# Where the V tiles live, when V and the expert weights load, and one score unit per slot: a fused attention and mixture-of-experts kernel

## The chip, the cores and the metric

The kernel runs on one core of a Trainium2 chip. The metric is device time in microseconds (us) of one execution. The core has TensorE (matmuls; PE, with PEld for its weight loads), VectorE (DVE), ScalarE (ACT), GpSimd (POOL) and SyncE (SP). Each works through its own instructions in order, and they wait for each other and for DMAs on semaphores. A DMA that GpSimd, ScalarE or SyncE issues is carried out by 16 DMA engines that all share.

## The reference

Block-causal attention for 8 batches of 8 heads, 576 positions and 64 dimensions (blocks of 64), whose output (4608 tokens of 512) goes through a mixture of 8 experts, of which each token takes two, by noisy logits:

```python
scores = scale * np.matmul(q, k.transpose(0, 1, 3, 2))
mask = block_i >= block_j
scores = np.where(mask, scores, -1000000000.0)
attn = np.exp(scores - np.max(scores, axis=-1, keepdims=True))
attn = attn / (np.sum(attn, axis=-1, keepdims=True) + 1e-09)
x = np.matmul(attn, v)          # then heads side by side, (4608, 512)
...
noisy_logits = x @ w_gate + np.log1p(np.exp(x @ w_noise)) * noise
top2 = np.argpartition(-noisy_logits, 2, axis=1)[:, :2]
top2_w = softmax of the two logits
...
for e in range(E):
    for k in range(2):
        mask = top2[:, k] == e
        h = np.maximum(x[mask] @ w1[e], 0.0)
        out[mask] += top2_w[mask, k, None] * (h @ w2[e])
```

w1 is 8 x 512 x 1024 and w2 is 8 x 1024 x 512; inputs and output are float32, the kernel's matmuls bfloat16.

## The kernel before

**Attention in groups and slots.** The 8 batches are taken two at a time, in 4 groups (g = 0 to 3), both batches of a group in the two halves of the partitions. A group is cut into UG = 26 slots: 13 score units for heads 0 to 3 (set 0) and 13 for heads 4 to 7 (set 1). A score unit (`score_unit`, L285) is a few matmuls of keys with queries into one of two PSUM buffers, and one exp by ScalarE (L302, or L313 for the last unit of a set) that empties it. Beside the score units, each slot has a list of other work, written down by hand: `at(slot, fn, ...)` puts a function into a slot, and `run(slot)` emits what stands there. The order of the program is the order on each engine. In a slot can stand the transposes of q and k of this group or the next (`transpose_qk`, copied out by VectorE or ScalarE), the products of exps and V (`av_tile`, L324, copied out by VectorE), the transposes of the finished rows (`x_transpose`), a router step (`router_step`), a load, or a scatter. In the loop of L794 the even slots emit two score units and then their own work, the odd slots only their work.

**V.** `load_v` (L210) loads V of a group into one of two tiles, `vt[g % 2]`, ten loads for a group, issued by GpSimd in slots 9 to 18 of the group before. The tiles have a column of ones (L722) that yields the sum of the exps. `xrs[g]` (L328), the finished rows of a group, comes from `xr_pool`, which has three buffers.

**Router and scatter.** For each group the router finds the two experts and a slot number for each token. `scatter` (L496) then writes the rows to a table in DRAM ordered by expert, xd[half], 18 indirect DMAs for a group, all issued by GpSimd; groups 0 and 1 make half 0, groups 2 and 3 half 1. The scatters of groups 0 to 3 stand in slots 52 to 63, 78 to 95, 101 to 114 and 118 to 135. Each is tied to a recent instruction (`pace[-1]`), so that they don't come too early.

**Experts.** From slot 104 on 16 blocks follow: one block is one half and one expert (`SEQ`, L627), 640 rows. Its rows come by a transposing DMA that SyncE issues (`load_x`, L515), which waits for all 36 scatters of that half. `layer1(b, fb)` (L567) is 8 steps of 8 matmuls and a relu by ScalarE; `layer2(b, c)` (L581) is 5 tiles of 8 matmuls. What a half's earlier experts contributed is stored to DRAM (yd, by a DMA that ScalarE issues) and gathered again later (`gather`, L609, GpSimd), added, and scattered to the output (L598). Layer 1, step 0, of block b + 1 stands before layer 2 of block b. With E1 = 4 the order is half 0 with experts 0 to 3, half 1 with experts 0 to 3, and then by turns, half 0 and half 1, with expert 4, 5, 6, 7. `XL` (L847) says in which step the rows of a later block are loaded, `WL` (L823) in which step a piece of an expert's weights; each step is followed by one `run(slot)` (slots 111 on).

**Weights.** An expert's weights are four DMAs of 512 KB (`load_w`, L220, k = 0 to 3), issued by GpSimd. Experts 0 and 1 go to the two buffers of `wE`, expert 2 to `wM`, expert 3 to `wL`. Expert 0 stands in slots 53 to 59, expert 1 in slots 80 to 92, expert 2 in slots 112 to 120, expert 3 in slots 124 to 133 (L811); experts 4 to 7 follow in the blocks. So on GpSimd's queue, from slot 52 on, all scatters, eight V loads and two half ones, and the weights of experts 0 to 3 stand one behind another.

Of the kernel before, what the change touches and what calls it, by code (L numbers as in the profile page):

```python
# [19 lines left out]
def kernel(  # L20
# [12 lines left out]
    nc = tc.nc  # L33
# [149 lines left out]
    kv = k.rearrange("b h s d -> (b h s d)").rearrange("(t p c) -> p t c", p=P, c=512)  # L183
    raws = {}
    vt = [v_pool.tile([P, TG, H, D + 1], BF16, name=f"vt{i}") for i in range(2)]
    hq = hq_pool.tile([P, 2 * FB * CAP], BF16)
    qT = hq[:, 0:73 * 64]
    kT = hq[:, 73 * 64:2 * 73 * 64]
# [20 lines left out]

    def load_v(g, idx, p0, n, tok):  # L210
        b, s0 = divmod(tok, S)
        nc.gpsimd.dma_start(out=vt[g % 2][p0:p0 + n, idx, :, 0:D],  # L212
                            in_=v[b, :, s0:s0 + n, :].rearrange("h s d -> s h d"))

    def v_loads(g):
# [107 lines left out]

    def av_tile(g, st, idx, part=None):  # L324
        esc, esc4 = escs[(g, st)]
        vb = vt[g % 2]
        if g not in xrs:
            xrs[g] = xr_pool.tile([P, TG, DR], BF16, tag="xr", name="xr")  # L328
            nc.gpsimd.memset(xrs[g][:, :, Dm + 2 * NREC:DR], 0.0)
            nc.gpsimd.tensor_copy(xrs[g][:, :, Dm + 4:Dm + 6].bitcast(I32)[:, :, 0], tokm[:, g, :])  # L330
        xr = xrs[g]
        if part != 1:
            avs_open[idx] = av_ps.tile([P, SET, D + 1], F32, tag="av", name="av")
        av = avs_open[idx]
        heads = range(SET) if part is None else range(2 * part, 2 * part + 2)
        if idx < 8:
            hf, ib = divmod(idx, 4)
            for hh in heads:
                for jt in range(ib + 1):
                    c = EO[jt] + (ib - jt) * P  # L340
                    nc.tensor.matmul(out=av[:, hh, :], lhsT=esc[:, hh, hf, c:c + P],  # L341
                                     rhs=vb[:, 4 * hf + jt, st * SET + hh, :], start=(jt == 0), stop=(jt == ib))
# [280 lines left out]
    GS = (2, 3, 5, 6)  # L623


    E1 = 4
    SEQ = [(h, e) for h in range(NH) for e in range(E1)]  # L627
    for e in range(E1, E):
        SEQ += [(0, e), (1, e)]
# [71 lines left out]
    def read_flags():  # L701
        rs["over"] = nc.values_load(flag_i[0:1, 0:1], min_val=0, max_val=1)

    pools = {}

    def load_later(e, k):
        load_w(pools["wL"], e, k)

    fl = keep.tile([P, 4, E], F32)
    flm = keep.tile([P, 1], F32)  # L710
    flag_i = keep.tile([P, 1], I32)
# [6 lines left out]
    nc.vector.tensor_copy(ident, ident_f)  # L718
    load_qk(0, (1,))
    load_nz()  # L720
    for i in range(2):
        nc.vector.memset(vt[i][:, :, :, D:D + 1], 1.0)  # L722
    load_qk(0, (2, 3))
    setup_pool()
# [9 lines left out]
    for g in range(NG):  # L734
# [6 lines left out]
        if not last:  # L741
            for nm, ch, i in (("q", 0, 14 if g else 19), ("k", 0, 17 if g else 22), ("q", "4B", 22), ("k", "4B", 21)):
                at(s0 + i, transpose_qk, g + 1, nm, ch)
            for i, (fn, *a) in enumerate(v_loads(g + 1)):
                at(s0 + 9 + i, fn, *a)
        if g == 0:
            at(s0 + 13, load_qk, 1, (2,))
            at(s0 + 16, load_qk, 1, (3,))
# [40 lines left out]
    at(UG + 4, clear_x, 0, UG + 3)  # L789
    at(2 * UG + 4, clear_x, 1, 2 * UG + 3)  # L790
    for k in range(4):
        at(2 * UG + 1 + 2 * k, load_w, wE, 0, k)
        at(3 * UG + 2 + 4 * k, load_w, wE, 1, k)
    for u in range(NG * UG):  # L794
        if u % 2 == 0:
            score_unit(*divmod(u, UG))
            score_unit(*divmod(u + 1, UG))
        run(u)
        if u == 3 * UG + 13:
            raws_up.close()  # L800
            ffn["x"] = raws_up.enter_context(tc.tile_pool(name="xgp", bufs=3, side="right", reuse_waits="tile"))
            ffn["rec"] = raws_up.enter_context(tc.tile_pool(name="recp", bufs=1, side="right", reuse_waits="tile"))
            wM = raws_up.enter_context(tc.tile_pool(name="wM", bufs=1, side="right", reuse_waits="tile"))
            at(3 * UG + 18, load_x, 0)
            at(3 * UG + 19, load_x, 1)
            at(3 * UG + 20, load_rec, 0)
            at(3 * UG + 21, load_x, 2)
            at(3 * UG + 22, load_x, 3)
            for k in range(4):
                at(4 * UG + (8, 10, 13, 16)[k], load_w, wM, 2, k)  # L810
                at(4 * UG + (20, 23, 26, 29)[k], load_later, 3, k)  # L811

    WL = {}

    def open_top(slot):
        if slot == NG * UG + 6:
            top.close()
            wL = pools["wL"] = top.enter_context(tc.tile_pool(name="wL", bufs=2, reuse_waits="tile"))
            ffn["y"] = top.enter_context(tc.tile_pool(name="yp", bufs=4, reuse_waits="tile"))
            ffn["yg"] = [ffn["y"].tile([P, Dm], BF16, name=f"yg{i}", bufs=1) for i in range(GB)]  # L820
            for i, pool in enumerate((wL, wE, wE, wM)):
                for k in range(4):
                    WL[4 + 2 * i + k // 2, (2, 6)[k % 2]] = (pool, 4 + i, k)  # L823

    slot = NG * UG
    at(slot + 14, read_rec, 0)
# [16 lines left out]
    for i in range(7):  # L843
        run(slot)
        slot += 1
        open_top(slot)
    XL = {(b, 1): b + 2 for b in range(2, NB - 2)}  # L847
    for fn, b, j in steps:
        fn(b, j)
        if fn is layer1:  # L850
            if (b, j) in XL:
                load_x(XL[b, j])
            if (b, j) == (3, 1):
                load_rec(1)
            if (b, j) == (4, 3):
                read_rec(1)
            if (b, j) in WL:
                load_w(*WL[b, j])
            if b in (1, E1 + 1) and j == 1:
                gather(b, 0)  # L860
            elif b < 2 * E1 and j in GJ and GJ.index(j) < LT[SEQ[b][1]]:
                gather(b, GJ.index(j))
            if 2 * E1 <= b + 1 < NB and j in GS and GS.index(j) < LT[SEQ[b + 1][1]]:
                gather(b + 1, GS.index(j))
        if fn is layer2 and 2 * E1 <= b + 1 < NB and j == order(b)[0] and LT[SEQ[b + 1][1]] > 4:
            gather(b + 1, 4)
            if b + 1 == NB - 1:
                nc.gpsimd.drain()  # L868
# [93 lines left out]
```

## Time and profile before

| | us |
|---|---|
| median of 14 runs | 457.01 |
| lowest and highest of them | 444.27, 475.29 |
| the profiled execution | 445.26 |
| its span, first to last instruction | 443.5 |
| mean granted TensorE clock in it | 0.96 |

The page tells of one execution: how long each engine was busy, in which stretches, and what it waited for. A line of the timeline has the start, the length, the engine, the line of the kernel, the operation, the tiles it writes and reads, how many were merged, and in brackets the idle time of the engine before it and what ended it. A group of instructions is written like this (busy time and mean ns of one, then idle time before it and its releaser):

```profile
L577 ACT ACTIVATE hq<-hp 128x640 bf16<-128x640 f32 x128 | 89.9, 703 | 64.5 <-PE hp L574 59.0
L302 ACT ACTIVATE esc<-sc 128x1024 bf16<-128x1024 f32 x96 | 92.5, 1023 | 11.0 <-PE sc L299 10.6
L499 POOL DMA_INDIRECT xd<-xr,slots x72 | 71.6, 994 | 31.6 <-issue 13.9
L212 POOL DMA_DIRECT2D vt<-in_v_dram x40 | 34.0, 874 | 9.6 <-PE av L355 5.1
```

The attention fills the span up to about 152 us, the 16 blocks of the experts the rest.

### The profile page before, as it was taken

What the parts mean: (1) busy time and instruction counts of PE and PEld (TensorE: products, weight loads), DVE (VectorE), ACT (ScalarE), POOL (GpSimd) and SP (SyncE); (2) the same over time, 40 slices, a digit from 0 to 9 for tenths busy, and PEclk for the clock granted to TensorE, in tenths of its full rate; (3) what the DMA queues carried; (4) which work ended last, traced back from release to release, by engine and by line L of the source; (5) the groups of instructions that cost most, each with busy time, mean ns of one, the idle gap of its engine ahead of it and who ended that gap; (6) DMA issues with size and microseconds to landing.
All of it is one profiled execution on the core that took longest, in us unless ns stands there. A gap on an engine that the chain in (4) does not pass through costs nothing. (4 is left out here: it accounts for less than half of the span.)

```text
span 443.5 us, 9826 instructions
## 1 busy us (share of the span) xinstructions
PE 402.3 (91%) x3952; PEld 250.1 (56%) x3952; DVE 158.0 (36%) x508; ACT 251.6 (57%) x343; POOL 251.4 (57%) x299
## 2 busy tenths in 40 slices
PE   2788987987977999997899999999999999999994
PEld 2456755755755766563555656656556456566561
DVE  1576778878869780001031000110201202302212
ACT  2997788789795155462445545545555455455140
POOL 8877362678878786883230304465357318666343
PEclk9969989989997899999799999999999999999999
DMA  8999999999978999999859399998997999734222
GB/s 132 173 128 171 217 205 183 218 254 164 127 187 186 217 241 261 224 197 230 124 156 179 72 172 171 175 207 197 212 222 197 117 203 239 209 128 161 72 86 106
DMA packets 134729, 78.93 MB, mean 178 GB/s; under 512 B 96033, under 2 KB 124451, under 8 KB 134676
## 3 DMA queue, kind: packets, MB, share of 16 engines
q0 software_dynamic: 70464, 56.05, 77.8%
q1 hardware_dynamic: 54132, 13.00, 18.5%
q10 hardware_dynamic: 10080, 9.18, 6.7%
q8 instruction: 33, 0.54, 0.6%
q14 instruction: 20, 0.16, 0.1%
HBM read 68.54 MB, written 33.13 MB: 229 GB/s over the span
## 5 line engine op out<-in xcount | busy, mean ns | idle before, releaser
L586 PE MATMUL yp<-w2sb,hq 128*128 128x512 bf16 x640 | 140.9, 379 | 0.8 <-DVE yo L596 0.8
L574 PE MATMUL hp<-xg,w1sb 128*128 128x320 bf16 x960 | 135.4, 302 | 4.4 <-ACT hq L577 4.4
L574 PEld LDWEIGHTS <-w1sb 128*128 128x128 bf16 x1024 | 100.9, 99 | 47.2 <-issue 4.6
L577 ACT ACTIVATE hq<-hp 128x640 bf16<-128x640 f32 x128 | 89.9, 703 | 64.5 <-PE hp L574 59.0
L596 DVE SCALAR_TENSOR_TENSOR yo<-yp,wrow,yg 128x512 f32<-128x512 f32 x46 | 34.5, 751 | 233.2 <-ACT ysb L591 188.8
L586 PEld LDWEIGHTS <-hq 128*128 128x128 bf16 x640 | 62.6, 98 | 74.0 <-issue 1.1
L302 ACT ACTIVATE esc<-sc 128x1024 bf16<-128x1024 f32 x96 | 92.5, 1023 | 11.0 <-PE sc L299 10.6
L598 POOL DMA_INDIRECT out_dram<-yo,trow x46 | 45.7, 994 | 83.6 <-DVE yo L596 69.5
L591 ACT ACTIVATE ysb<-yp,wrow 128x512 bf16<-128x512 f32 x70 | 48.1, 687 | 73.5 <-PE yp L586 71.5
L499 POOL DMA_INDIRECT xd<-xr,slots x72 | 71.6, 994 | 31.6 <-issue 13.9
L614 POOL DMA_INDIRECT yg<-yd,orow x48 | 49.5, 1032 | 52.1 <-ACT hq L577 25.2
L299 PE MATMUL sc<-hq 64*128 64x512 bf16 (+4 forms) x320 | 37.9, 325 | 13.1 <-ACT esc L302 10.9
L341 PE MATMUL av<-vt,esc 128*128 128x65 bf16 x640 | 32.8, 206 | 7.7 <-DVE xr L360 6.3
L212 POOL DMA_DIRECT2D vt<-in_v_dram x40 | 34.0, 874 | 9.6 <-PE av L355 5.1
L341 PEld LDWEIGHTS <-esc 128*128 128x128 bf16 x640 | 26.0, 105 | 17.1 <-DVE xr L360 12.4
L360 DVE TENSOR_TENSOR xr<-av,rden 128x256 bf16<-128x256 f32 x72 | 30.6, 425 | 2.6
L299 PEld LDWEIGHTS <-hq 64*128 64x128 bf16 x320 | 12.7, 98 | 25.9 <-issue 16.1
L256 PE MATMUL tp<-ident,raw 128*64 128x128 bf16 x512 | 23.9, 246 | 2.5 <-DMA raw<-in_q_dram 1.9
L269 ACT ACTIVATE hq<-tp 128x1024 bf16<-128x1024 bf16 (+1 forms) x20 | 17.0, 852 | 13.5 <-PE tp L256 6.8
L256 PEld LDWEIGHTS <-raw 128*64 128x64 bf16 x512 | 18.2, 125 | 8.2 <-issue 3.3
L262 DVE COPY hq<-tp 128x1024 bf16<-128x1024 bf16 (+1 forms) x24 | 14.3, 597 | 7.9 <-PE tp L256 5.6
L359 DVE RECIPROCAL rden<-av 128x4 f32<-128x4 f32 x72 | 12.8, 178 | 7.2 <-PE av L355 3.3
(122 smaller groups left out, 220.0 us busy)
## 6 DMA issues: line engine op xcount, KB each, us to landing
yd<-ysb ACTq DMA_DIRECT2D x70, 128.0 KB, 3.6
w1sb<-in_moe_w_dram POOLq DMA_DIRECT2D x16, 512.0 KB
w2sb<-in_moe_w_dram POOLq DMA_DIRECT2D x16, 512.0 KB, 8.3
vt<-in_v_dram POOLq DMA_DIRECT2D x32, 128.0 KB, 8.0
raw<-in_q_dram POOLq DMA_DIRECT2D x9, 256.0 KB, 7.3
raw<-in_k_dram POOLq DMA_DIRECT2D x9, 256.0 KB
xd<-zero SPq DMA_DIRECT2D x16, 132.0 KB, 6.1
raw<-in_q_dram POOLq DMA_DIRECT2D x1, 1152.0 KB, 12.8
```

The source lines that it names most:

```text
L256: nc.tensor.transpose(to[64 * hf:64 * hf + 64, :, r, :], raw[:, (t0, t1)[hf], r * 64:(r + 1) * 64], ident)
L299: nc.tensor.matmul(out=sc[:, hf, off:off + z - a], lhsT=kT[sl, c0 + jt * P:c0 + jt * P + P], rhs=qT[sl, c0 + a:c0 + z], start=True, stop=True)
L302: ins = nc.scalar.activation(out=esc[:, hh, :, piece * 512:(piece + 1) * 512], in_=sc, func=AF.Exp, scale=scale)
L341: nc.tensor.matmul(out=av[:, hh, :], lhsT=esc[:, hh, hf, c:c + P], rhs=vb[:, 4 * hf + jt, st * SET + hh, :], start=(jt == 0), stop=(jt == ib))
L499: ins = nc.gpsimd.indirect_dma_start(out=xd[half].bitcast(I32), out_offset=bass.IndirectOffsetOnAxis(ap=slots[:, g * TG + idx, i:i + 1], a ...
L574: nc.tensor.matmul(out=hp[:, n, 0:NW], lhsT=w1sb[:, db, fb * P:(fb + 1) * P], rhs=xgs[b][:, db, n * NW:(n + 1) * NW], start=(db == 0), sto ...
L577: ins = nc.scalar.activation(out=hs[b][:, fb, :].rearrange("p (n w) -> p n w", n=2), in_=hp[:, :, 0:NW], func=AF.Relu)
L586: nc.tensor.matmul(out=yp, lhsT=hs[b][:, fb, c * P:(c + 1) * P], rhs=w2sb[:, fb, :], start=(fb == 0), stop=(fb == FB - 1))
L591: ins = nc.scalar.activation(out=ysb, in_=yp, func=AF.Copy, scale=w)
L596: nc.vector.scalar_tensor_tensor(out=yo, in0=yp, scalar=w, in1=ygs.pop((b, c)), op0=ALU.mult, op1=ALU.add)
L598: ins = nc.gpsimd.indirect_dma_start(out=out, out_offset=bass.IndirectOffsetOnAxis(ap=trow[half][:, e, c:c + 1], axis=0), in_=yo, in_offse ...
L614: ins = nc.gpsimd.indirect_dma_start(out=yg, out_offset=None, in_=yd[half][0:e * CAP, :], in_offset=bass.IndirectOffsetOnAxis(ap=orows[hal ...
```

## The change

V: there are now four entries in `vt`. Groups 0 and 3 use the first tile, group 2 the second, and group 1 a tile from `xr_pool`, the same buffer that later holds the rows of group 2. V of group 3 is loaded in slots 46 to 50 and not in 61 to 70. Expert 0's weights move from slots 53 to 59 to slots 61 to 70, expert 1's from 80 to 92 to 73 to 82. Each slot emits one score unit and then its work. Half 1 begins after three experts and not after four (E1 = 3): block 3 is half 1 with expert 0. Expert 3's weights are no longer loaded in slots 124 to 133, but in blocks 3 and 4, and those of experts 4 to 7 one block later than before. The rows of block 3, and then of block 4 and the records of half 1, are loaded in steps 4, 5 and 6 of block 2, and the records of half 1 are read in block 3.

```diff
     vt = [v_pool.tile([P, TG, H, D + 1], BF16, name=f"vt{i}") for i in range(2)]
+    v1 = xr_pool.tile([P, TG, DR], BF16, tag="xr", name="xr")
+    v1 = v1.rearrange("p t c -> p (t c)")[:, 0:TG * H * (D + 1)]
+    vt.insert(1, v1.rearrange("p (t h d) -> p t h d", t=TG, h=H))
+    vt.append(vt[0])
...
-        nc.gpsimd.dma_start(out=vt[g % 2][p0:p0 + n, idx, :, 0:D],
+        nc.gpsimd.dma_start(out=vt[g][p0:p0 + n, idx, :, 0:D],
...
-        vb = vt[g % 2]
+        vb = vt[g]
...
-    E1 = 4
+    E1 = 3
...
-    for i in range(2):
+    for i in range(3):
         nc.vector.memset(vt[i][:, :, :, D:D + 1], 1.0)
...
-                at(s0 + 9 + i, fn, *a)
+                at((9 + i, UG + 9 + i, UG + 20 + i // 2)[g], fn, *a)
...
-        at(2 * UG + 1 + 2 * k, load_w, wE, 0, k)
-        at(3 * UG + 2 + 4 * k, load_w, wE, 1, k)
+        at(2 * UG + 9 + 3 * k, load_w, wE, 0, k)
+        at(2 * UG + 21 + 3 * k, load_w, wE, 1, k)
     for u in range(NG * UG):
-        if u % 2 == 0:
-            score_unit(*divmod(u, UG))
-            score_unit(*divmod(u + 1, UG))
+        score_unit(*divmod(u, UG))
         run(u)
...
-            at(3 * UG + 22, load_x, 3)
             for k in range(4):
                 at(4 * UG + (8, 10, 13, 16)[k], load_w, wM, 2, k)
-                at(4 * UG + (20, 23, 26, 29)[k], load_later, 3, k)
...
-            for i, pool in enumerate((wL, wE, wE, wM)):
+            for i, pool in enumerate((wL, wL, wE, wE, wM)):
                 for k in range(4):
-                    WL[4 + 2 * i + k // 2, (2, 6)[k % 2]] = (pool, 4 + i, k)
+                    WL[3 + 2 * i + k // 2, (2, 6)[k % 2]] = (pool, 3 + i, k)
...
-    XL = {(b, 1): b + 2 for b in range(2, NB - 2)}
+    XL = {(2, 4): 3, (2, 5): 4}
+    for b in range(3, NB - 2):
+        XL[b, 1] = b + 2
...
-            if (b, j) == (3, 1):
+            if (b, j) == (2, 6):
                 load_rec(1)
-            if (b, j) == (4, 3):
+            if (b, j) == (3, 3):
                 read_rec(1)
...
-            elif b < 2 * E1 and j in GJ and GJ.index(j) < LT[SEQ[b][1]]:
+            elif b < 9 and j in GJ and GJ.index(j) < LT[SEQ[b][1]]:
...
-            if 2 * E1 <= b + 1 < NB and j in GS and GS.index(j) < LT[SEQ[b + 1][1]]:
+            if 9 <= b + 1 < NB and j in GS and GS.index(j) < LT[SEQ[b + 1][1]]:
```

The other changed lines follow from these (the last gather of a block, the helper `load_later` that falls away).

More of the change, by code (lines that the diff above doesn't have):

```diff
@@ L702, in read_flags @@
         rs["over"] = nc.values_load(flag_i[0:1, 0:1], min_val=0, max_val=1)
-    pools = {}
-    def load_later(e, k):
-        load_w(pools["wL"], e, k)
     fl = keep.tile([P, 4, E], F32)
@@ L817, in open_top @@
             top.close()
-            wL = pools["wL"] = top.enter_context(tc.tile_pool(name="wL", bufs=2, reuse_waits="tile"))
+            wL = top.enter_context(tc.tile_pool(name="wL", bufs=2, reuse_waits="tile"))
             ffn["y"] = top.enter_context(tc.tile_pool(name="yp", bufs=4, reuse_waits="tile"))
             ffn["yg"] = [ffn["y"].tile([P, Dm], BF16, name=f"yg{i}", bufs=1) for i in range(GB)]
-            for i, pool in enumerate((wL, wE, wE, wM)):
+            for i, pool in enumerate((wL, wL, wE, wE, wM)):
                 for k in range(4):
-                    WL[4 + 2 * i + k // 2, (2, 6)[k % 2]] = (pool, 4 + i, k)
+                    WL[3 + 2 * i + k // 2, (2, 6)[k % 2]] = (pool, 3 + i, k)
     slot = NG * UG
@@ L860 @@
                 gather(b, 0)
-            elif b < 2 * E1 and j in GJ and GJ.index(j) < LT[SEQ[b][1]]:
+            elif b < 9 and j in GJ and GJ.index(j) < LT[SEQ[b][1]]:
                 gather(b, GJ.index(j))
-            if 2 * E1 <= b + 1 < NB and j in GS and GS.index(j) < LT[SEQ[b + 1][1]]:
+            if 9 <= b + 1 < NB and j in GS and GS.index(j) < LT[SEQ[b + 1][1]]:
                 gather(b + 1, GS.index(j))
-        if fn is layer2 and 2 * E1 <= b + 1 < NB and j == order(b)[0] and LT[SEQ[b + 1][1]] > 4:
+        if fn is layer2 and 9 <= b + 1 < NB and j == order(b)[0] and LT[SEQ[b + 1][1]] > 4:
             gather(b + 1, 4)
```

## The prediction

> **What bounds the kernel now.** I read the page first, for the share of each engine, then a table of six stages, then who TensorE waits for, and then the order of events around the two places where it does wait.
>
> ```profile
> span 443.5 us, 9826 instructions
> PE 402.3 (91%) x3952; PEld 250.1 (56%) x3952; DVE 158.0 (36%) x508; ACT 251.6 (57%) x343; POOL 251.4 (57%) x299
> ```
>
> TensorE is idle for 41.2 us of 443.5. The stages (first column the stretch, then its length and the busy time of PE, PEld, DVE, ACT, POOL, and the granted clock) say where:
>
> ```profile
> 78.50:112.00 33.50, 28.78 (x576) 20.38 (x576) 26.29 (x88) 28.14 (x38) 27.31 (x31) 0.95 1.12 208
> 112.00:152.00 40.00, 33.84 (x659) 25.29 (x660) 31.93 (x103) 24.63 (x33) 32.04 (x36) 0.87 1.05 182
> 152.00:205.30 53.30, 53.30 (x333) 31.54 (x330) 13.08 (x53) 27.92 (x44) 39.38 (x41) 1.00 1.05 229
> 205.30:229.40 24.10, 19.66 (x105) 10.97 (x104) 2.91 (x4) 8.95 (x13) 6.13 (x6) 0.86 0.81 146
> ```
>
> From 152 us on, TensorE never rests, except in block 3 (205.3 to 229.4). Layer 1, step 1, starts at 298.7 in block 8 and at 316.0 in block 9: an undisturbed block takes 17.3 us. From that step of block 3 to that of block 4 it is 24.1 us, so 6.8 us are lost there. In an attention group (78.5 to 112) PE, ACT and DVE each work 26 to 29 of 33.5 us: no engine is the bound, they wait on each other. TensorE's waits name the two places:
>
> ```profile
> PE sc L299 <- ACT esc L302: 10.9, 18, 1.6
> PE hp L574 <- ACT hq L577: 4.4, 1, 4.4
> ```
>
> The second one is in block 3. Its cause is one row further up. SyncE may load an expert's rows of half 1 only when all 36 scatters of groups 2 and 3 have landed, and GpSimd issues those one after the other to the end:
>
> ```profile
> 141.91 0.97 POOL L499 DMA_INDIRECT xd<-xr,slots  x1 [0.30 <-issue]
> ...
> 195.07 0.81 POOL L232 DMA_DIRECT2D w2sb<-in_moe_w_dram  x1
> 196.19 1.00 POOL L499 DMA_INDIRECT xd<-xr,slots  x1 [0.30 <-DMA w2sb<-in_moe_w_dram]
> 197.50 0.99 POOL L499 DMA_INDIRECT xd<-xr,slots  x1 [0.31 <-issue]
> ```
>
> ```profile
> 204.91 6.65 SPq L519 DMA_TRANSPOSE xg<-xd  x2
> ```
>
> The last scatter starts at 197.50; the load of block 4's rows starts at 204.91. A store that ScalarE issues shares a completion semaphore with that load and waits for it until 210.9, so block 3 stands still from 207.6 to 212.05, and the matmuls that follow run at half clock (0.50 granted from 212.05 to 216.3, their median 470 ns against 299).
>
> **Part by part.**
>
> *V and weights in another order.* In the stretch from 79.5 (slot 52) to 115, GpSimd issues 18 scatters, 4 pieces of expert 0 and 10 pieces of V. The V issues take 0.70 to 0.97 us each. V of group 3 moves to slots 46 to 50, where GpSimd idles (8.94 us before the scatter at 79.52); expert 0 takes V's old place, expert 1 comes before and among the first scatters of group 1. So group 1's scatters start at slot 78 (its last router step ends at 111.9) and not at 115.22: about 3 us earlier. For TensorE that is worth nothing by itself: no row has it waiting for vt or for a weight, and block 0's rows landed at 150.4 for a start at 152.1. The cover of that is thin (1.7 us) and grows by 3. V of group 2 no longer waits for group 0's readers (5.09 us of GpSimd idle at 54.77). The row buffer that V of group 1 borrows is free 7 slots (9 us) before group 2 writes it. The third memset of ones costs 0.12 us at the start.
>
> *Expert 3's weights leave the scatter queue.* The gaps between scatter starts are 1.28 us, and 2.05, 2.07, 2.10 and 2.09 us where a piece of expert 3 lies between (one of them before a gather): 3.2 us less in all. Group 2's first scatter cannot profit fully: it was issued at 141.91 straight after the one before, but its router's last step ends at 140.3, so 140.6 is the earliest, 1.3 us gained. The last scatter then starts at 197.5 - 3.2 - 1.3 = 193.0. It lands later by 7.2 to 8.0 us where expert 3's pieces are in the rings (186 to 198 us) and by 3.6 to 4.8 us where fewer loads are (147 to 162 us); with the weights gone I take 4.8: 197.8.
>
> *Three experts and not four before half 1 begins.* This is the expensive part. Block 3 is now the first of half 1 and needs those rows in layer 1, step 0, which TensorE takes before layer 2 of block 2. That step starts at 195.6 in this trace, 12.0 us ahead of where it stops now (207.6). The load begins some 0.3 us after the landing and takes 6.0 us to land (204.91 to 210.9; 144.45 to 150.43 for block 0): 204.1. TensorE would stand from 195.6 to 204.1, 8.5 us, and nothing can pass it, since its order is fixed. Adding the same 2.1 us for the half clock, 10.6 us, against 6.8 lost today: **+3.8 us**. With the landing of 3.6 it is +2.6; with 8.0 and 3.4 us of clock loss (6.9 us at half, as at 131.0 to 137.9) it is 11.7 + 3.4 - 6.8 = +8.3. If attention ends earlier, group 2's scatters and block 0 move together and the wait stays. The pieces of expert 3 now issue in blocks 3 and 4, 17 us ahead of block 6, where GpSimd idles (8.02 us before 227.90); block 3 has no gathers. The records are loaded behind two row loads (6.83 us of SyncE between 204.91 and 211.74) and land 6.9 us later, at 198.1 + 6.8 + 6.9 = 211.8; layer 2 of block 3 wants them some 20 us after TensorE goes on at 204.1 (8.6 of layer 2, 8.7 of layer 1, 1.7 of the first tile). Nothing here.
>
> *One score unit per slot.* Order before: two score units, then the work of two slots. The place where it hurts:
>
> ```profile
> 93.76 0.30 PE L341 MATMUL av<-vt,esc 128*128 128x65 bf16 x4
> 95.11 0.39 PE L299 MATMUL sc<-hq 64*128 64x512 bf16 x2 [1.05 <-ACT esc L302]
> 96.03 0.39 PE L299 MATMUL sc<-hq 64*128 64x64 bf16 x4 [0.52 <-ACT esc L302]
> 96.35 0.42 PE L341 MATMUL av<-vt,esc 128*128 128x65 bf16 x8
> ```
>
> ScalarE has a copy of keys, three router steps and two exps (0.92 us apart) in a row there, and TensorE wants two score buffers at once while the AV tile of 96.35 could have run. With one unit per slot the AV tile goes between: the second wait goes and the first halves, about 1.1 us. It recurs in groups 1 and 3 (1.05 + 0.52 at 60.7; 1.62 + 0.52 at 127.0), so **-3.3 us** in all. Bounds: all of these waits, -5.3; on the other side the hand-overs from TensorE to ScalarE double, and ScalarE's waits for scores (10.6 us in 18 waits) could double too, +10.6. I take -3.3, because the rows of just this place show it.
>
> After each of those three waits the clock is at half (96.9 to 100.3, 62.8 to 66.2 and 131.0 to 137.9: 13.7 us). If it were kept up, up to 13.7 / 2 = 6.8 us more would be gained. I take none of it, since group 0 and the tail drop as well, with other causes.
>
> The Trainium skill, "TensorE: Matmul & The Clock Gate", Part 1, says that the clock halves after at least one idle window of about 3.4 us, and comes back after one such busy window. By that rule waits of 1 us would drop no clock and their removal would bring none back, while the 8.5 us wait in block 3 is sure to; these rows show drops after far shorter waits than the rule asks for. By the rule the sum would be that above, by the rows up to 6.8 us lower.
>
> Sum: 3.8 - 3.3 + 0.1 = +0.6 us on an execution of 445.26 us (span 443.5 and 1.8 around it). That execution is among the quickest; the median of the 14 runs is 457.01, and of the 12 us between I know only that waits on DMAs and clock drops are what can grow. A slower DMA lengthens block 3's new wait in full, so I add 0.9: **458.5**.
>
> **Rivals.**
> 1. *The wait in block 3 decides* (slower). The scatters land as slowly as now (8.0) and the single score units gain nothing, because ScalarE is short of work when each long slot starts with one exp and not two. +8.3: 465.3. For it: GpSimd issues back to back from 141.9 on and 36 scatters at 1.28 us are 46 us whatever else moves. Against: the weights that filled the rings are gone. It decides once the two parts together cost 4 us more than in the forecast.
> 2. *Attention decides* (faster). All three waits go, and the clock stays up: -5.3 - 6.8 + 2.6 = -9.5: 447.5. For it: the drops follow the waits each time. Against: the clock also drops at 144.7, in the tail, where waits for VectorE of 0.84 and 0.36 us come first, which this change leaves alone, and after 97 ScalarE idles for 1.38 and 0.72 us more, so that it isn't all that holds a group.
> 3. *The reordering does nothing*: V and weights hide anyway; that is already in the forecast at zero, and gives it alone 457.
>
> **How the numbers follow.** About 1% (4.6 us) is what a measurement of this kernel can tell. Forecast, the two parts nearly cancelling, own range 454 to 463: 0.40, of which 0.08 lies above +1%. Rival 1: 0.30, rival 2: 0.30. So faster 0.30, same 0.32, slower 0.38. The range has to reach both rivals' times, with a bit beyond for the upper: 447 to 469.
>
> **What would show it.** Block 3: a wait of layer 1, step 0, for xg of 7 to 12 us, with half clock after it, and the last scatter near 193 minus any shift of block 0's start. Group 2: no second wait for an exp near 96, the group under 33 us. Wrong if block 3's rows are there in time (then the scatters were not bound by GpSimd), if a group takes longer than 33.5, or if another block waits for weights of expert 3.

## The result and the profile after

| | median, us | lowest to highest |
|---|---|---|
| before, 47 runs | 457.17 | 443.55 to 484.70 |
| after, 10 runs | 458.56 | 456.40 to 460.46 |

The changed kernel is slower: 1.0267 times before, interval 1.0236 to 1.0298. The medians lie closer than that because many runs of before and few of after were disturbed, and the ratio is of undisturbed runs alone. So the median comes out at the predicted 458.5 by chance; the forecast itself, two parts that nearly cancel, is not what happened. The profiled execution took 460.24 us, 14.98 more than the one of before (445.26).

The page of after, its first line and the busy time of the engines:

```profile
span 458.3 us, 9847 instructions
PE 404.8 (88%) x3952; PEld 251.1 (55%) x3952; DVE 158.4 (35%) x509; ACT 252.8 (55%) x343; POOL 250.1 (55%) x299
```

TensorE's work grew by 2.5 us (402.3 to 404.8) and its idle time by 12.3 (41.2 to 53.5). Who it waits for, with the sum, the number and the longest of the waits:

```profile
PE hp L579 <- DMA xd<-xr,slots: 11.3, 1, 11.3
PE sc L304 <- ACT esc L307: 9.6, 17, 1.5
PE hp L579 <- DMA xg<-xd: 8.3, 1, 8.3
```

The 4.4 us wait for a relu (hq) of before is gone, the waits for exps fell from 10.9 to 9.6 (with those of the last score unit of a set, which have a line of their own, from 11.3 to 11.0), and two waits for rows of layer 1 have come: 8.3 us in block 3, which the prediction has, and 11.3 us in block 0, which it doesn't. TensorE's timeline around the two, and the same stretches by engine (length; busy time of PE, PEld, DVE, ACT, POOL; granted clock; DMA share; GB/s):

```profile
148.59 1.05 PE L396 MATMUL lg<-wgn,xT 128*128 128x16 bf16 x36
...
160.93 3.36 PE L579 MATMUL hp<-xa,w1sb 128*128 128x320 bf16 x12 [11.29 <-DMA xd<-xr,slots]
...
215.53 2.31 PE L579 MATMUL hp<-xg,w1sb 128*128 128x320 bf16 x8 [8.31 <-DMA xg<-xd]
```

```profile
149.60:160.90 11.30, 0.04 (x2) 0.00 (x1) 2.98 (x12) 0.53 (x3) 8.73 (x9) 0.64 0.61 170
160.90:182.10 21.20, 21.17 (x114) 12.19 (x115) 9.49 (x40) 9.28 (x15) 16.63 (x19) 0.87 1.02 202
199.50:227.90 28.40, 20.09 (x105) 10.87 (x104) 1.50 (x2) 9.07 (x13) 9.30 (x10) 0.82 0.66 145
```

Attention is done 2.4 us sooner (149.64 against 152.08), and then TensorE stands for 11.3 us. GpSimd works for 8.7 of them: until 153.3 it is still issuing scatters. The difference of the two spans, read off the starts of layer 1, step 1, adds up:

| | before | after | us |
|---|---|---|---|
| block 0 starts | 152.1 | 160.9 | +8.8 |
| from there to step 1 of block 1 | 18.5 | 21.2 | +2.7 |
| the block with the stop, to the next one's step 1 | 24.1 | 28.5 | +4.4 |
| the stop of 1.0 in block 10, a wait of TensorE for VectorE at 350 | 1.0 | 0 | -1.0 |
| sum; difference of the spans | | | +14.9; +14.8 |

The 2.7 are half clock: after the wait 0.50 is granted until 166.4, for 5.5 us.

Why are the rows late? GpSimd's timeline of after, from the loads of q and k of group 3 on:

```profile
64.73 0.99 POOL L212 DMA_DIRECT2D raw<-in_q_dram  x1 [1.34 <-PE av L346]
...
66.39 0.90 POOL L217 DMA_DIRECT2D vt<-in_v_dram  x1 [0.39 <-DMA raw<-in_k_dram]
67.54 1.69 POOL L217 DMA_DIRECT2D vt<-in_v_dram  x2 [0.25 <-DMA vt<-in_v_dram]
69.79 0.98 POOL L212 DMA_DIRECT2D raw<-in_k_dram  x1 [0.56 <-DMA vt<-in_v_dram]
70.77 2.58 POOL L217 DMA_DIRECT2D vt<-in_v_dram  x3
77.99 3.66 POOL L217 DMA_DIRECT2D vt<-in_v_dram  x4 [4.65 <-DMA raw<-in_q_dram]
87.09 0.87 POOL L217 DMA_DIRECT2D vt<-in_v_dram  x1 [5.44 <-DMA raw<-in_k_dram]
...
93.34 1.09 POOL L504 DMA_INDIRECT xd<-xr,slots  x1 [1.09 <-DVE noisy L415]
```

A load of V has no business with q. But the V load that waits until q has landed is the eighth issue after it (behind q: V is 1 to 3, k is 4, V is 5 to 7), and the one that waits for k is the eighth after k. So it looks as if the issues of GpSimd take eight completion semaphores in turn, and each must find the one before it done (a semaphore is the counter by which a DMA reports that it has landed). The counts show the eighth; the semaphores themselves are not seen. q and k take 13 and 17 us to land. The V loads at 77.99 and 87.09 stand in the queue for that, and group 0's scatters stand behind them: the first goes out at 93.34 and not at 79.52. From there on 36 scatters at 1.285 us and 8 pieces of weights at 0.8 are 52.6 us of issuing without a break, and there are breaks:

```profile
117.70 0.79 POOL L237 DMA_DIRECT2D w1sb<-in_moe_w_dram  x1
...
118.67 1.59 POOL L237 DMA_DIRECT2D w2sb<-in_moe_w_dram  x2
120.21 1.46 POOL L237 DMA_DIRECT2D w1sb<-in_moe_w_dram  x2
...
125.82 1.00 POOL L504 DMA_INDIRECT xd<-xr,slots  x1 [0.62 <-ACT esc L307]
128.41 0.98 POOL L504 DMA_INDIRECT xd<-xr,slots  x1 [1.59 <-ACT esc L307]
...
130.97 0.97 POOL L504 DMA_INDIRECT xd<-xr,slots  x1 [1.59 <-DMA w2sb<-in_moe_w_dram]
...
133.74 0.80 POOL L237 DMA_DIRECT2D w2sb<-in_moe_w_dram  x1 [1.79 <-DMA w1sb<-in_moe_w_dram]
...
136.79 1.00 POOL L504 DMA_INDIRECT xd<-xr,slots  x1 [2.25 <-DMA xd<-xr,slots]
```

These breaks follow the same count. The five pieces of weights issued from 117.70 to 121 are each followed, as the eighth issue behind, by one of the five that wait (125.82, 128.41, 130.97, 133.74, 136.79; the releasers named in the rows differ, the count fits all five). So those pieces were 8 to 16 us in the rings, that is, handed to the DMA engines and not yet landed, while issues 1.28 us apart come round to the same place after some 10 us. In before the weights go out piece by piece among the scatters, one lands in 8.3 us (the median), and nothing waits for it. Group 1's last scatter starts at 152.3 (before: 140.6), and SyncE's load of block 0's rows at 154.86 (144.5).

### The profile page after: what moved, and what is told of

It reads as the page before. It is cut to its first block, busy times and chain, and to the rows that moved or that the text cites. A ratio compares the mean times of both kernels' runs of the same rounds, so it can differ in the third digit from the quotient of the medians.

```text
span 458.3 us, 9847 instructions
## 1 busy us (share of the span) xinstructions
PE 404.8 (88%) x3952; PEld 251.1 (55%) x3952; DVE 158.4 (35%) x509; ACT 252.8 (55%) x343; POOL 250.1 (55%) x299
## 5 line engine op out<-in xcount | busy, mean ns | idle before, releaser
L591 PE MATMUL yp<-w2sb,hq 128*128 128x512 bf16 x640 | 142.4, 382 | 0.0
L307 ACT ACTIVATE esc<-sc 128x1024 bf16<-128x1024 f32 x96 | 93.6, 1026 | 8.6 <-PE sc L304 8.3
L304 PE MATMUL sc<-hq 64*128 64x512 bf16 (+4 forms) x320 | 39.6, 316 | 11.0 <-ACT esc L307 9.6
L217 POOL DMA_DIRECT2D vt<-in_v_dram x30 | 25.2, 846 | 21.8 <-DMA raw<-in_q_dram 8.8
L346 PE MATMUL av<-vt,esc 128*128 128x65 bf16 x480 | 25.4, 210 | 3.5 <-DVE xr L365 3.5
L579 PE MATMUL hp<-xa,w1sb 128*128 128x320 bf16 x64 | 11.6, 354 | 11.3 <-DMA xd<-xr,slots 11.3
```

The lines of the kernel that those rows point to most:

```text
L304: nc.tensor.matmul(out=sc[:, hf, off:off + z - a], lhsT=kT[sl, c0 + jt * P:c0 + jt * P + P], rhs=qT[sl, c0 + a:c0 + z], start=True, stop=True)
L307: ins = nc.scalar.activation(out=esc[:, hh, :, piece * 512:(piece + 1) * 512], in_=sc, func=AF.Exp, scale=scale)
L579: nc.tensor.matmul(out=hp[:, n, 0:NW], lhsT=w1sb[:, db, fb * P:(fb + 1) * P], rhs=xgs[b][:, db, n * NW:(n + 1) * NW], start=(db == 0), sto ...
L591: nc.tensor.matmul(out=yp, lhsT=hs[b][:, fb, c * P:(c + 1) * P], rhs=w2sb[:, fb, :], start=(fb == 0), stop=(fb == FB - 1))
```

## The experiments

The theory: V of group 3 ahead of the scatters, and the weights close together behind them, make the scatters of half 0 late, and that costs block 0 some 11.5 us; the E1 and score-unit parts do about what was forecast. The rivals: one of the two alone is the cause (A: V only, or weights only, as the run has it), or the time lies in E1 = 3. Kernels named a_ are after with something put back, kernels named b_ are before with one part of the change or a new edit. On two of the chips attention took 20 to 30 us longer in every kernel, before included (it ended at 171 to 182 us, elsewhere at 147 to 152), so absolute times are compared only among runs with the short attention.

**V and weights: each put back, and both.** `after_again` is the changed kernel itself, on another chip. `a_v3_back` puts V of group 3 back:

```diff
-                at((9 + i, UG + 9 + i, UG + 20 + i // 2)[g], fn, *a)
+                at((9 + i, UG + 9 + i, 2 * UG + 9 + i)[g], fn, *a)
```

`a_w_back` puts the weights back, and `a_vw_back` (three runs) does both:

```diff
-        at(2 * UG + 9 + 3 * k, load_w, wE, 0, k)
-        at(2 * UG + 21 + 3 * k, load_w, wE, 1, k)
+        at(2 * UG + 1 + 2 * k, load_w, wE, 0, k)
+        at(3 * UG + 2 + 4 * k, load_w, wE, 1, k)
```

`a_v3_half` loads five of the ten V pieces early and the rest at `2 * UG + 9 + i`. `b_v_early` is before with the V part alone (the borrowed buffer, and V of group 3 in slots 46 to 50).

> The changed kernel once more, so that its traces stand beside the next three on one chip. Theory (both moves together delay block 0 by delaying the scatters of groups 0 and 1): first scatter 12 us or more behind that of the kernel with both moves taken back, group 1's last 8 to 12 us behind; 2 to 3% over before.

> The changed kernel, with V of group 3 loaded in slots 61 to 70 again, all else as changed. Theory (the ten V loads of group 3 stand on GpSimd's queue in front of group 0's scatters, and wait there for their completion semaphores while the DMA rings are full): the first scatter starts at 79 to 81 us, not at 93.3; group 1's last at 139 to 143, not at 152.3; block 0 starts at 150 to 152, not at 160.9; the span falls from 458.3 to 445 to 449. Rival A (the weights of experts 0 and 1, put close together, hold up group 1's scatters): block 0 still starts at 157 or later, the span stays over 453. Rival B (one score unit per slot changes what the scatters are tied to): no change, 457 to 460.

> The changed kernel, with the weights of experts 0 and 1 in their old slots (53 to 59, 80 to 92). Theory: the first scatter stays at 93, block 0 starts within 4 us of 160.9, the span stays at 455 to 463. Rival A: group 1's last scatter moves from 152.3 to 146 or earlier, block 0 to 154 or earlier, the span to 452 or less.

> The changed kernel, with five of the ten V loads of group 3 in slots 61 to 70 (idx 5 on) and five left in slots 46 to 48. Theory: the first scatter lies between, at 80 to 88 us, and block 0 starts between 150 and 156; span 445 to 454. Rival A and rival B: as the changed kernel, 93 and 160.9, 456 to 460.

> The kernel before, with the V part alone: V of group 1 in a row buffer, V of group 3 in slots 46 to 50; weights, score units and the order of experts as before. Theory: the first scatter moves from 79.5 to 90 to 95 us, block 0 from 152.1 to 158 to 165, and the span from 443.5 to 452 to 460. Rival A: first scatter and block 0 within 2 us of before, span 442 to 446. Rival B: the same as rival A.

> The changed kernel, with V of group 3 and the weights of experts 0 and 1 all in their old slots; one score unit per slot and half 1 after three experts stay. Theory, amended (the delay of block 0 is made by the two moves together: V in front holds up the first scatter by 13 us, and the eight weight pieces that are then issued close together hold up the scatters of group 1): first scatter 77 to 80 us, group 1's last at 138 to 142, block 0 at 149.5 to 152, span 443 to 448, the wait of block 3 still there (27 to 30 us from its step 1 of block 2 to that of block 3). Rival (one score unit per slot alone makes block 0 late, since its rows and scatters are tied to it): block 0 at 154 or later, as in the two runs that take one move back.

> The changed kernel with V of group 3 and the weights of experts 0 and 1 all in their old slots, once more, on another chip (on the first one every kernel took 30 to 50 us more). Theory (both moves together delay block 0): first scatter 77 to 80 us, group 1's last at 138 to 142, block 0 at 149.5 to 152, span 443 to 448, block 3's wait still there (26 to 30 us from step 1 of block 2 to step 1 of block 3). Rival (one score unit per slot makes block 0 late by itself): block 0 at 154 or later.

> The changed kernel with V of group 3 and the weights of experts 0 and 1 in their old slots. Theory: block 0 begins 8 to 11 us earlier than in the changed kernel of the same chip, within 1.5 us of the end of attention; block 3's wait stays; time within 1% of before. Rival (one score unit per slot, or the borrowed row buffer, makes block 0 late): less than 3 us earlier.

Measured, in us (the ratio is to before):

| kernel | first scatter | group 1's last | load of block 0's rows | block 0 starts, wait | span | ratio |
|---|---|---|---|---|---|---|
| before | 79.5 | 140.6 | 144.5 | 152.1, none | 443.5 | |
| after | 93.3 | 152.3 | 154.9 | 160.9, 11.3 | 458.3 | 1.0267 [1.0236, 1.0298] |
| after_again | 93.4 | 151.1 | 153.7 | 159.8, 11.3 | 456.9 | 1.0181 [1.0011, 1.0352] |
| a_v3_back | 76.9 | 144.7 | 147.2 | 154.6, 4.4 | 452.1 | 1.0060 [0.9984, 1.0135] |
| a_w_back | 92.1 | 144.4 | 148.4 | 154.6, 6.5 | 450.0 | 1.0058 [0.9989, 1.0128] |
| a_v3_half | 80.2 | 146.0 | 148.5 | 155.0, 5.2 | 451.6 | 1.0055 [1.0006, 1.0103] |
| b_v_early | 92.6 | 144.8 | 149.5 | 157.7, 5.8 | 455.9 | none |
| a_vw_back_3 | 75.8 | 140.6 | 146.4 | 153.2, 5.8 | 448.7 | 1.0015 [0.9921, 1.0110] |

The rows come from more than one chip: `a_v3_back`, `a_w_back`, `a_v3_half` and `b_v_early` ran on one, `after_again` and `a_vw_back_3` on another, and for before and after the record names none. With V and weights in their old places group 1's last scatter starts at 140.6 on the second of them and at 141.2 on the first (`b_e1_3_3`, below), so the rows can be set side by side to about 1 us.

Group 1's last scatter tells it. With both parts back it is 140.6, as in before; with the weights' order alone 144.7, with early V alone 144.4, with both 151.1 and 152.3. Each alone costs 4 us, together they cost 10.5 to 11.7. So neither theory nor rival was right as put. The theory expected of `a_v3_back` a scatter at 139 to 143 and a span of 445 to 449, and got half of the way; and of `a_w_back`, block 0 within 4 us of 160.9, which fell. Its rival there, the weights, came nearer, but early V keeps its 4 us without them. `a_v3_half` came out as forecast (first scatter, block 0 and span). `b_v_early` had the first scatter and the span as forecast and block 0 at 157.7, just under the 158; its traced execution took 457.71 us, one of four from 446.63 to 459.89, so what early V alone costs in time isn't settled.

The time of that scatter can be taken apart: the first scatter, 52.6 us of scatters and weights, the ten V issues where they stand between (34.0 / 40 = 0.85 us each, 8.5 in all), and what is left, the breaks.

| kernel | first | + issues | + V | = without breaks | measured | breaks |
|---|---|---|---|---|---|---|
| before | 79.5 | 52.6 | 8.5 | 140.6 | 140.6 | 0 |
| a_vw_back_3 | 75.8 | 52.6 | 8.5 | 136.9 | 140.6 | 3.7 |
| a_v3_back | 76.9 | 52.6 | 8.5 | 138.0 | 144.7 | 6.7 |
| a_w_back | 92.1 | 52.6 | 0 | 144.7 | 144.4 | 0 |
| after_again | 93.4 | 52.6 | 0 | 146.0 | 151.1 | 5.1 |
| after | 93.3 | 52.6 | 0 | 145.9 | 152.3 | 6.4 |

Early V starts the scatters 13 us late and saves 8.5 us of issues behind the first. With the weights close together there are breaks of 5 to 7 us; in their old places there are none in two of the three kernels. In the third, `a_vw_back_3`, nearly all of the 3.7 us is one scatter at 86.33, which stands for 3.37 us: the eighth issue after a load of k (67.81). So scatters that start early meet k's turn and win little. In `a_v3_back` the scatters go out early and meet the semaphore instead of V (GpSimd's timeline):

```profile
85.78 0.97 POOL L504 DMA_INDIRECT xd<-xr,slots  x1 [1.37 <-DMA raw<-in_k_dram]
...
129.12 1.01 POOL L504 DMA_INDIRECT xd<-xr,slots  x1 [2.67 <-DMA xd<-xr,slots]
```

The first line is again the eighth issue after k's (67.80), now a scatter, and the second the eighth after a piece of weights (115.50): the place in the order waits, whatever stands there. In `a_v3_half`, with five V pieces early, k's eighth is a scatter at 85.06, and that waits 3.74 us. That it is the issuer that waits is stated by the Trainium skill, "DMA: Bandwidth & Descriptors", section "Anatomy of one DMA — SWDGE (gpsimd) path": DMA engines do not wait on semaphores, the issuing sequencer does, before it dispatches. The waits of 4.65, 5.44 and 3.74 us on GpSimd agree; the turn of eight, and with it the wait for an unrelated earlier DMA, is read from these traces.

The same chip ran `after_again` and `a_vw_back_3`: putting both back brings 8.2 us of span (456.9 to 448.7) and block 0 6.6 us earlier. The expectation was 8 to 11, within 1.5 us of the end of attention; its rival's, less than 3, fell as well. The rest of the wait stays (TensorE's timeline of `a_vw_back_3`):

```profile
153.19 7.40 PE L579 MATMUL hp<-xa,w1sb 128*128 128x320 bf16 x32 [5.84 <-DMA xa<-xd]
```

There attention ends at 147.4, before the rows are there: their load starts at 146.4 although group 1's last scatter is at 140.6 as in before. `a_vw_back` on one of the two other chips gave 0.9987 [0.9919, 1.0055], and its second run on the other no ratio (medians 484.38 and 482.71); where attention takes over 20 us longer the rows come in time anyway, and these two can't tell the theories apart.

**E1 = 3 alone.** `b_e1_3` is after with V, weights and pairs of score units back, so that what is left of the change is E1 = 3 with expert 3's weights in the blocks, and the borrowed buffer for V of group 1:

```diff
-        score_unit(*divmod(u, UG))
+        if u % 2 == 0:
+            score_unit(*divmod(u, UG))
+            score_unit(*divmod(u + 1, UG))
         run(u)
```

> The kernel before with the order of experts alone changed: half 1 after three experts, expert 3's weights in blocks 3 and 4 (V in the four-entry list, but loaded in its old slots; two score units in every second slot). Prediction's step: 3.8 us more than before, from a wait of layer 1, step 0, of block 3 for its rows; from step 1 of block 2 to step 1 of block 3 26 to 30 us where an undisturbed block has 17.3 and block 3 had 24.1 one block later. Span 446 to 449. Rival (without the weights in its queue GpSimd ends its scatters in time): 18 to 22 us, span 438 to 442.

> The kernel before with the order of experts alone changed, once more, on another chip. Prediction's step: 3.8 us more than before; 26 to 30 us from step 1 of block 2 to step 1 of block 3, span 446 to 449. Rival: 18 to 22 us there, span 438 to 442.

> The kernel before with the order of experts alone changed. Prediction's step: block 0 as in before (152 to 154), 26 to 29 us from step 1 of block 2 to step 1 of block 3, against 24.1 one block later in before; 0.5 to 1.5% over before. Rival (that part of the change is worth nothing or brings time): 22 us or less there, ratio 1.00 or under.

The ratios are 1.0169 [1.0040, 1.0298] and, in the third run, 1.0137 [1.0079, 1.0195]; the second run, on a chip with long attention, gave none. The third's span is 447.4, 3.9 over before; its ratio puts the cost at 3.5 to 8.7 us. SyncE's and TensorE's timelines in it:

```profile
198.85 6.14 SPq L524 DMA_TRANSPOSE xg<-xd  x2
```

```profile
205.12 2.31 PE L579 MATMUL hp<-xg,w1sb 128*128 128x320 bf16 x8 [8.68 <-DMA xg<-xd]
```

Layer 1, step 0, of block 3 waits 8.68 us for rows whose load started at 198.85, and the block takes 27.8 us against 24.1 (26.2 and 28.0 in the other two runs). This part is a loss by itself.

**One score unit per slot alone.** `b_single` is before with the loop of after (the diff above the other way round).

> The kernel before with one score unit per slot, nothing else. Prediction's step: attention ends 3.3 us earlier (last matmul before block 0 at 149 to 150, not at 152.1). Block 0's rows land at about 150.4, so block 0 starts at 149.5 to 151.5 and the span falls by 1 to 3 us, 440.5 to 442.5. Rival (the hand-overs cost as much as they bring): attention ends at 151.5 or later, span 443 to 446.

> The kernel before with one score unit per slot alone, once more, on another chip. Prediction's step: the last matmul before block 0 ends at 149 to 150 and not at 152.1; block 0 starts at 149.5 to 151.5; span 440.5 to 442.5. Rival: 151.5 or later, span 443 to 446.

> The kernel before with one score unit per slot alone. Prediction's step: 1 to 3 us less than before (ratio 0.993 to 0.998); the run on the last chip gave 0.984. Rival: no gain, 0.999 to 1.005.

Only the second run gives a ratio: 0.9843 [0.9725, 0.9960], on a chip with long attention. The first has medians of 491.21 against 496.71 and no ratio. In the third, attention ends at 149.3, 2.8 us before the trace of before, and block 0 then waits 3.90 us for its rows and starts at 153.2, 1.1 later; its medians are 457.88 against 454.88, without a ratio. Its traced execution is the longest of four (467.67). There is no borrowed buffer and no moved V in it, and block 0 starts at 153.2 just as in `a_vw_back_3`; half clock follows the wait in both (21.1 and 21.4 us to step 1 of block 1, 18.5 in before). So attention does end sooner, and that is paid out only where the rows of half 0 are there as well. On the chip with long attention they are (`b_single_2` has no wait for xa).

**The store's semaphore.** The prediction read block 3's stop in before as a store that shares a completion semaphore with the load of block 4's rows. `b_lane` and `b_lane_single` (with single score units too) give that load a further dependence, on an instruction that is long done by then, so that it should fall to another turn:

```diff
         xgs[b] = xg
+        if b == E1:
+            tc.add_manual_dep(ins.ins, pace[-1], SYNC_DEP, reason="after the stores of block 1")
```

(the two lines stand ahead of `xgs[b] = xg`).

> The kernel before, with the load of block 4's rows tied to layer 1, step 1, of block 2, which is long over when that load can start; its completion semaphore is then another one than that of the last store of block 2. The prediction's reading of before (ScalarE stands still because that store waits for the load's semaphore): the idle 4.4 us in block 3 and the half clock after it go, 17.3 to 18 us from block 3 to block 4, span 436.5 to 438.5. Rival (the wait is one for data or for full rings, and stays): 23 to 25 us, span 442 to 445.

> The kernel before with one score unit per slot and with the load of block 4's rows tied to layer 1, step 1, of block 2, so that the last store of block 2 no longer shares its semaphore. If both readings hold: no wait in block 3, 17.3 to 18 us from it to block 4, block 0 at 149.5 to 151.5, span 434 to 438, 2 to 3% under before. If the store's wait was one for data or for rings: 23 to 25 us in block 3, span 440 to 443.

> The kernel before with one score unit per slot and the other semaphore for the load of block 4's rows: no wait in block 3 (17.3 to 18 us to block 4), and 5 to 7 us less than with one score unit alone, that is 2 to 3% under before. Rival: the wait comes back elsewhere, same time as with one score unit alone.

`b_single_2` and `b_lane_single` ran on the same chip. In `b_single_2` the store stands from about 230 to 232.99, ScalarE's relu behind it, and TensorE behind that (its timelines of ScalarE, then TensorE):

```profile
232.99 0.33 ACTq L593 DMA_DIRECT2D yd<-ysb  x1
233.36 1.30 ACT L577 ACTIVATE hq<-hp 128x640 bf16<-128x640 f32 x2 [3.10 <-DMA xg<-xd]
```

```profile
229.36 2.34 PE L574 MATMUL hp<-xg,w1sb 128*128 128x320 bf16 x16
234.11 8.35 PE L574 MATMUL hp<-xg,w1sb 128*128 128x320 bf16 x48 [2.41 <-ACT hq L577]
```

In `b_lane_single` the same two blocks (3, then 4) follow each other in 17.3 us, without a stop, though that load runs at 230.67 just the same:

```profile
215.42 8.86 PE L576 MATMUL hp<-xg,w1sb 128*128 128x320 bf16 x64
232.75 8.86 PE L576 MATMUL hp<-xg,w1sb 128*128 128x320 bf16 x64
```

That the load holds up the store, and that it needn't, is shown; which semaphore each takes is not seen in the trace. Ratios: `b_lane` 0.9777 [0.9662, 0.9892], which rests on two of its four executions; `b_lane_single` none there (medians 475.99 against 482.71), and on another chip, in `b_lane_single_2`, 0.9902 [0.9816, 0.9987]. Both beat before; which of the two is better stays open, as they never ran on one chip. The forecast of 17.3 to 18 us from block 3 to block 4 held in `b_lane_single` alone. `b_lane` has 19.8 us there, with a wait of 1.26 for VectorE, and `b_lane_single_2` 22.0, with 1.91 for block 4's rows, whose load starts only at 213.90, and 2.43 for VectorE; its gain is 1% and not the 2 to 3% forecast. What moved that load is open.

**Scatters first, weights after.** If the issuing queue were all, moving expert 1's weights behind group 1's scatters would bring the rows early enough for single score units. `best` is `b_lane_single` with that:

```diff
-        at(3 * UG + 2 + 4 * k, load_w, wE, 1, k)
+        at(3 * UG + 18 + k, load_w, wE, 1, k)
```

> The kernel before with one score unit per slot, the other semaphore for the load of block 4's rows, and expert 1's weights behind group 1's scatters (slots 96 to 99, not 80 to 92). Theory (block 0 starts when the rows of half 0 have landed, and those wait for group 1's last scatter on GpSimd's queue): the last scatter of group 1 starts 3 us earlier, at about 137 to 138, block 0's rows land at 146 to 148.5, block 0 starts at 148.5 to 150; no wait of over 1 us at blocks 0 and 3; 2 to 3% under before. Rival (the landing depends on the rings and not on the queue): rows land at 150 or later, 1% under before as the run without the weights' move.

It is slower than before, 1.0313 [1.0164, 1.0462]. Group 1's last scatter does start at 136.6, 4 us ahead of before, as forecast. But the weights are then issued together, just ahead of the load of the rows (GpSimd, SyncE and TensorE in its timeline):

```profile
137.59 1.55 POOL L232 DMA_DIRECT2D w1sb<-in_moe_w_dram  x2
139.08 1.55 POOL L232 DMA_DIRECT2D w2sb<-in_moe_w_dram  x2
```

```profile
139.37 12.57 SPq L519 DMA_TRANSPOSE xa<-xd  x1
```

```profile
158.12 2.31 PE L576 MATMUL hp<-xa,w1sb 128*128 128x320 bf16 x8 [8.59 <-DMA xa<-xd]
```

The load takes 18.7 us to land, against 6.0 in before and in `b_lane_single_2`, which differs in the weights' move alone. The theory of the queue alone falls with this: what is in the rings when the load of the rows starts counts too. The rival had the late landing right, and not its time of 1% under before. The trace is of the longest of its executions (474.69 of 454.54 to 474.69), and block 0 at 158.1 is 6.0 us later than in before, less than half of what the ratio says; the rest was not followed up.

## Why the prediction was wrong

**The steps that failed** are two terms of the sum. The first is V and weights, put at 0: "For TensorE that is worth nothing by itself". On one chip, putting both back takes 8.2 us off the span (one traced execution each; medians 457.79 and 451.04): block 0 starts 6.6 us earlier and the block with the stop is 2.1 shorter, while the half clock behind block 0's start costs 0.6 more. So this term was about +8 where 0 stood. The argument went wrong in two places. "V of group 3 moves to slots 46 to 50, where GpSimd idles (8.94 us before the scatter at 79.52)" took an idle engine for a free queue. The loads of q and k from 63.74 and 68.90 were still landing then, and an issue put there becomes their eighth follower and stands until they are done. And "group 1's scatters start at slot 78 ... about 3 us earlier" counted instructions on the queue and left out the waits between them: with the first scatter at 93.3 and 18 scatters and 4 weights to go, group 1's can't start before 93.3 + 23.1 + 3.2 = 119.6, 4.4 us later than the 115.22 of before, though the V issues are gone from between; it started at 121.97.

The second is the -3.3 of single score units, counted in full although block 0 can't start before its rows have landed. The prediction had seen how little stood against this: "The cover of that is thin (1.7 us)", but it let the cover grow by 3 and had no rival in which it fails. The cover shrank instead. With V and weights in their old places attention ends at 147.4 and 149.3 (`a_vw_back_3`, `b_single_3`), and block 0 still starts at 153.2, 1.1 later than in before, with 2.9 and 2.6 us of half clock behind it: about +4 where -3.3 stood. In `b_lane_single_2`, also with single units, block 0 starts at 150.5 with 1.7 us behind, about 0 in all, so this term is not settled to a few us. With +2.3 for the block with the stop and -1.0 for the one in block 10, the first two terms, 8.2 and 4.0, make 13.5 us; `after_again` less before is 13.4.

**E1 = 3**: right in mechanism, and in size with some luck. Forecast 8.5 us of wait and +3.8 us, by itself 8.68 and a span 3.9 longer; in after 8.31 and +4.4, of which 2.1 go with V and weights. But the last scatter by itself started at 196.2 and not at 193.0, and its landing was seen 2.6 us later where 4.8 was taken, so that two misses cancel: the load started at 198.85, against 198.1.

**One score unit per slot**, as to attention itself: the size is about right, the wait is not the one named. Attention ends 2.4 us sooner in after and 2.8 in the third `b_single` (over all runs with the short attention at 147.4 to 150.2 with single units, at 151.8 to 152.4 with pairs). The place that the prediction named, in TensorE's timeline of after:

```profile
93.03 0.39 PE L304 MATMUL sc<-hq 64*128 64x512 bf16 x2 [0.28 <-ACT esc L307]
93.36 0.42 PE L346 MATMUL av<-vt,esc 128*128 128x65 bf16 x8
93.94 0.40 PE L304 MATMUL sc<-hq 64*128 64x64 bf16 x4 [0.17 <-ACT esc L307]
```

The AV tile now goes between the two, and 1.05 and 0.52 us of waits are 0.28 and 0.17. From that unit of group 2 to the same of group 3 it is 32.4 us, under the 33 that the prediction asked for. But part of the wait has moved one unit ahead, in group 1 and in group 3:

```profile
60.37 0.39 PE L304 MATMUL sc<-hq 64*128 64x320 bf16 x4 [1.01 <-ACT esc L307]
...
124.55 0.40 PE L304 MATMUL sc<-hq 64*128 64x320 bf16 x4 [1.51 <-ACT esc L307]
```

With that unit the three places cost 5.3 us before and 4.1 after, 1.2 less and not 3.3. What fell more are the waits of AV tiles for VectorE, first before, then after:

```profile
PE av L341 <- DVE xr L360: 6.3, 13, 0.8
PE av L346 <- DVE xr L365: 4.2, 8, 1.5
```

Why they fell was not tested. And the gain doesn't reach the end of the span: attention that ends sooner only waits longer for rows.

**The clock**, of which 0 of up to 6.8 us was taken: between 10 and 150 us half clock is granted for 27.3 us in before and for 20.5 in after. The rule that the prediction quoted ("TensorE: Matmul & The Clock Gate", Part 1) fits the long waits of 11.3 and 8.3 us: half clock sets in 3.1 and 3.5 us after they begin and lasts 13.7 and 10.2 us. The stretches at 62.8 and 96.9 in before followed waits of about a microsecond and are not there in after; but `b_e1_3_3` has the same waits as before near 96, 1.05 and 0.52 us, and keeps the full clock behind them. So what brings these short stretches stays open.

**The rivals**: the first had the sign right and the wrong place; block 3 costs +4.4 and not +8.3, and nothing in it is about block 0. Of the second, attention does end sooner, but the waits for exps hardly fell, half clock comes elsewhere in attention, and the kernel is slower. The third, that V and weights do nothing, is refuted by the 2 x 2 of the runs.

**Open**: why block 0's rows come so late with both parts back. Group 1's last scatter is then where it is in before, but the load of the rows starts 5.8 us after it and not 3.8. And why attention is 20 to 30 us longer on two of the chips.

## What to carry to other kernels

Before an issue moves into idle time of an engine, look at what is still landing from that engine's queue and at what stands behind: the issue can wait for a transfer it has nothing to do with, and everything behind it waits too. Two moves that each cost little in the end can cost more together where they fill the same queue, so run each alone and both. A faster stage pays only if the next stage's input is earlier too; and a short, urgent load should not start just behind bulk loads. A gain in a wait is not a gain in time before you have looked for where the wait went.

## What was not expected of the hardware

- An issue by GpSimd waits for the eighth issue before it to land (4.65 and 5.44 us in after, 3.74 in `a_v3_half`, 1.37 in `a_v3_back`, 0.62 to 2.25 behind five pieces of weights in after; a V load, a scatter or a piece of weights, wherever the count falls). This is read from the counts.
- The transposing load of 640 rows took 18.7 us to land behind four 512 KB loads issued within the 3 us around its start, and 6.0 us without them (one execution each).
- The same program's attention differs between chips: from group 2 on, a group takes 38 to 47 us on two of them and 32 to 34 on the others, while a block of an expert without a stop takes 17.3 us on all.
